# First batch of a packed-attention mixture-of-experts kernel: earlier splits, four hidden blocks as split products, and batch 1's key scores behind six items instead of two

## The chip, the cores and the metric

The kernel runs on one core of a Trainium2 chip. The metric is the device time of one execution in microseconds. Its engines are TensorE (PE, with its weight loads PEld), VectorE (DVE), ScalarE (ACT), GpSimd (POOL) and SyncE (SP, a queue of loads and stores).

## The reference

For each of 8 batches and 8 heads (576 tokens, head width 64) 32 packing queries `p` attend over keys `k` and values `v`; then the tokens' queries `q` attend over these 32 packed rows. The result (4608 x 512) goes through a layer of 8 experts, of which each token takes the best.

```python
p_packed = sm_attn(p, k, v)          # 32 rows for each head
out = sm_attn(q, p_packed, p_packed)
x = out.transpose(0, 2, 1, 3).reshape(4608, 512)
logits = (x / norm(x)) @ en.T / tau  # 8 experts
e = argmax(logits); gate = softmax(logits)[e]
y = gate * (relu(x @ w1[e]) @ w2[e]) # 512 -> 1024 -> 512
```

## The kernel before, in words

The kernel guesses one expert for a whole batch, works with that expert's weights, and would do the tokens that chose another in a rest loop. It never forms `x`: with the probabilities AT (for each group of four heads 128 packed rows by 576 tokens) and G = packed rows times w1 (128 x 1024 for each group), the hidden layer is relu(G^T AT). A batch's feed-forward, `ffn`, is 16 items `hidden(hf, f)`: two halves of 288 tokens and eight blocks f of 128 hidden columns. Then come `h4`, the leftover rows' second layer (tokens beyond 512, L924), and four row blocks of the second layer (L940).

Products come in two forms. A split product takes each operand as a high part (a cast to fp32r) and a low part (the remainder) and sums three products, high x high, high x low, low x high: an item has two groups, so six products (L893). A plain fp32 product takes one instruction for each group and no splits (`first_half`, L872), which needs only `g32` (G before its split) and `ats` (AT before its split).

`split` makes such a pair: a cast on ACT (L274), and a subtraction on POOL or DVE (L275). `split_g` does one of four blocks of G (column half fc, group g), `split_w2` one of eight blocks of w2 (L785, L786), `high` and `low` the two parts of AT for a half (L619, L623).

The attention of batch b + 1 runs in between: key tiles are transposed on DVE (`flip`, L285 to L287), key scores on PE (L260), maximum and exponential (L350, L355), p1 turned (L370) and copied (L381, L384), values (L390), query tiles transposed (L290, L294). `route` computes for each of five token blocks the squares and logits (L680, L689, L696) from AT and `ppx`, packed rows with 16 logits columns behind them, split too (`rows_split`, `logits_split`).

In the first batch all of this is started from a cold state, and a table sets the order. `PLAN[n + 1]` is what is emitted behind step n of `ffn`: s is a step of the first batch's softmax (its order in `ORDS`), G a `split_g`, a a step of batch 1's attention, w a `split_w2`, q and r steps of the first batch's logits and route. `ENG` says which of the subtractions go to POOL (p) and which to DVE (v): places 0 to 5 are S0, S1, N0, N1, L0, L1, places 6 to 9 the four `split_g`. All engines execute in the order emitted.

Banks set further waits: four PSUM banks of tag `pf` hold items until the second copy on DVE (L898, and L903 in the second half) has read them, two double banks of tag `pb` serve scores, turns and route. Six buffers `nat` hold loaded tiles until they are transposed.

Of the kernel before, what the change touches and what calls it, by code (L numbers as in the profile page):

```python
# [18 lines left out]
HB = 4  # L19
# [4 lines left out]
def kernel(  # L24
# [16 lines left out]
    NG = H // HB  # L41
# [230 lines left out]
    def split(dst, src, eng=nc.gpsimd):  # L272

        nc.scalar.copy(dst[0], src)  # L274
        eng.tensor_tensor(out=dst[1], in0=src, in1=dst[0].bitcast(F32), op=ALU.subtract)  # L275
# [278 lines left out]
    def att2(x, after=None, first=False, early=False):  # L554

        def eng(name, hf):
            i = ("S0", "S1", "N0", "N1", "L0", "L1").index(name + str(hf))
            return nc.gpsimd if first and ENG[i] == "p" else nc.vector

# [72 lines left out]
        def softmax():  # L632
# [4 lines left out]
            if first:  # L637
# [3 lines left out]
                groups = {"": both, "a": slice(0, 1), "b": slice(1, 2)}  # L641
                order = [(names[t[0]], int(t[1]), groups[t[2:]]) for t in ORDS.split()]
            for step, hf, *gs in order:
# [135 lines left out]
    def split_w2(x):  # L779
        f = len(x.w2s)  # L780
        if f == NF:
            return
        t = sb.tile([P, 2, DM], F32R, name="w2s", tag="w2s", bufs=NF)
        raw = x.w2r[f // 2][:, f % 2, :]
        nc.scalar.copy(t[:, 0], raw)  # L785
        nc.gpsimd.tensor_tensor(out=t[:, 1], in0=raw, in1=t[:, 0].bitcast(F32), op=ALU.subtract)  # L786
        x.w2s.append(t)

    PASSES = ((0, 0), (0, 1), (1, 0))

    def split_g(x):
        fc, g = x.gs // NG, x.gs % NG
        x.gs += 1
        split(
            [x.G[:, a, g, fc * 512 : fc * 512 + 512] for a in range(2)],
            x.g32[fc][:, g],
            nc.gpsimd if ENG[5 + x.gs] == "p" else nc.vector,
        )
# [32 lines left out]
    def ffn(x, store, late=False, after=None, end=False):  # L831
# [34 lines left out]
        opened = {}  # L866

        def first_half(f, g):

            if g == 0:  # L870
                opened[f] = ps.tile([P, 512], F32, name="pf", tag="pf")
            nc.tensor.matmul(  # L872
                opened[f][:, :HS], x.g32[f // 4][:, g, f % 4 * P : f % 4 * P + P],
                x.ats[0][:, g], start=(g == 0), stop=(g == NG - 1),
            )

        def hidden(hf, f):
            cs = slice(hf * HS, (hf + 1) * HS)

            assert not late or hf == 0 or x.soft and x.gs >= NG * (f // 4 + 1)  # L880
            if late and hf == 0:
                for g in range(f in opened, NG):
                    first_half(f, g)
                pf = opened[f]
            else:
                pf = ps.tile([P, 512], F32, name="pf", tag="pf")
                ops = [
                    (x.G[:, a, g, f * P : (f + 1) * P], x.AT[:, m, g, cs])
                    for g in range(NG)
                    for a, m in PASSES  # L890
                ]
                for n, (w, r) in enumerate(ops):
                    nc.tensor.matmul(pf[:, :HS], w, r, start=(n == 0), stop=(n == len(ops) - 1))  # L893
            yield
            n = HS if hf == 0 else 512 - HS
            cs = slice(hf * HS, hf * HS + n)
            nc.scalar.activation(hT[:, 0, f, cs], pf[:, :n], AF.Relu)  # L897
            nc.vector.scalar_tensor_tensor(  # L898
                out=hT[:, 1, f, cs], in0=pf[:, :n], scalar=0.0,
                in1=hT[:, 0, f, cs].bitcast(F32), op0=ALU.max, op1=ALU.subtract,  # L900
            )
            if hf:
                nc.vector.tensor_scalar(  # L903
                    out=h4[:, f], in0=pf[:, n:HS], scalar1=0.0, scalar2=None, op0=ALU.max
                )
            if f % 2 and not late:
                split_w2(x)
# [9 lines left out]
        for hf in range(2):  # L917
            for f in range(NF):
                yield from hidden(hf, f)
# [13 lines left out]
        for c in range(4):  # L933

            w = 256 if end and c == 3 else 512
            for at in range(0, 512, w):
                pf = ps.tile([P, 512], F32, name="pf", tag="pf")
                for f in range(NF):
                    for i, (a, m) in enumerate(PASSES):
                        nc.tensor.matmul(  # L940
# [254 lines left out]
    def store_main(b):  # L1195
# [24 lines left out]
    GATE = 18  # L1220


    ORDS = "U0a B0a S0a X0a U0b B0b T0a S0b X0b T0b N0a N0b R0a U1 B1 S1 X1 R0b T1 N1 R1 H1 L1 H0 L0"
    ENG = "pvpppppppp"

    PLAN = (
        "qssq", "sssssssss", "sss", "ss", "ss", "ssG", "", "sG", "ssa", "ssa",
# [82 lines left out]
    with tc.If(n_rest > 0):  # L1312
        with tc.For_i(0, B, 1) as b:
            nb = nc.values_load(rest_i[0:1, ds(b, 1)], min_val=0, max_val=S)
            with tc.If(nb > 0):
                x = Batch()
# [43 lines left out]
                for c in range(NC5):  # L1360
                    for hf in range(2):
                        a = acc[hf][:, c] if c < 4 else acc[0][64 * hf : 64 * hf + 64, 4]
# [38 lines left out]
```

## Time and profile before

| | |
|---|---|
| median of 3 runs | 445.36 us (444.05 to 445.59) |
| profiled execution | 444.3 us, span from first to last instruction 442.6 us |
| PE busy | 430.8 us, 97% of the span |
| DVE, ACT, POOL busy | 303.3, 203.6, 150.2 us |
| mean granted clock of TensorE | 0.996 of full speed |
| HBM traffic | 78.00 MB read, 9.44 MB written |

PE is the engine that is nearly always busy. Its records overlap (a product starts while the one before it still drains), so distances between starts, not busy times, tell how fast it works. The chain that ended last is 89% PE and 6% DMA; the DMA part lies in the first 23 us, before the first G.

### The profile page before, as it was taken

How to read it: one execution, taken by the hardware profiler on the slowest of the kernel's cores; microseconds unless marked ns; L12 is line 12 of the kernel's file. 1: busy time of each engine (PE TensorE's matmuls, PEld its weight loads, DVE VectorE, ACT ScalarE, POOL GpSimd, SP SyncE). 2: the span in 40 equal slices, each digit the busy share in tenths (PEclk: the TensorE clock that was granted, in tenths of full speed). 3: DMA queues.
4: the chain of work that ended last, by engine and by line, in shares of the span. 5: the costliest groups of instructions: out<-in, count | busy, mean ns of one | idle time of the engine just before them, and what ended most of it. 6: DMA issues, size and time to landing. Idle time of an engine off the chain costs nothing.

```text
span 442.6 us, 10441 instructions
## 1 busy us (share of the span) xinstructions
PE 430.8 (97%) x3762; PEld 339.4 (77%) x3763; DVE 303.3 (69%) x1006; ACT 203.6 (46%) x477; POOL 150.2 (34%) x201
## 2 busy tenths in 40 slices
PE   8799999999999999999999999999999999999994
PEld 6537768798787978879687977879687886879784
DVE  5568759669965899469883799558994698535400
ACT  2457632773237723465127723366235751466110
POOL 2538645342404441152504523044501534035000
PEclk9999999999999999999999999999999999999998
DMA  7999988877985479944995389843998206500011
GB/s 208 290 282 286 232 213 325 246 180 204 321 301 141 110 216 360 275 113 138 298 364 143 88 231 353 268 128 102 241 386 243 79 1 220 221 26 24 15 48 54
DMA packets 40267, 88.22 MB, mean 199 GB/s; under 512 B 10312, under 2 KB 19848, under 8 KB 40208
## 3 DMA queue, kind: packets, MB, share of 16 engines
q1 hardware_dynamic: 31920, 57.96, 46.2%
q0 software_dynamic: 8000, 29.43, 18.3%
q8 instruction: 32, 0.52, 0.5%
q14 instruction: 27, 0.22, 0.2%
q10 hardware_dynamic: 288, 0.08, 0.1%
HBM read 78.00 MB, written 9.44 MB: 198 GB/s over the span
## 4 chain that ended last, share of the span: by engine, by line
PE 89%; DMA 6%; DVE 2%; ACT 1%; SPq 1%; issue 0%; DVEq 0%; ACTq 0%
PE pf L940 41%; PE pf L893 21%; PE pf L924 6%; PE pt L680 6%; PE pt L260 4%; PE pt L810 3%; PE pt L390 3%; DMA nat<-in_v 2%; DMA nat<-in_q 2%; PE pt L370 1%; DMA w1t<-in_moe_w 1%; PE pf L853 1%; DVE hT L898 1%; PE pt L853 1%; PE pf L872 0%; SPq L201 0%
## 5 line engine op out<-in xcount | busy, mean ns | idle before, releaser
L940 PE MATMUL pf<-w2s,hT 128*128 128x512 f32 (+1 forms) x792 | 189.1, 390 | 0.0
L940 PEld LDWEIGHTS pf<-w2s,hT 128*128 128x128 f32 x792 | 142.1, 188 | 37.4 <-issue 6.7
L786 POOL TENSOR_TENSOR w2s<-w2r,w2s 128x512 fp32r<-128x512 f32 x64 | 82.6, 1292 | 178.3 <-ACT w2s L785 176.6
L893 PE MATMUL pf<-AT,G 128*128 128x288 f32 x720 | 105.0, 299 | 0.1
L893 PEld LDWEIGHTS pf<-AT,G 128*128 128x128 f32 x720 | 97.5, 188 | 5.1 <-issue 2.3
L897 ACT ACTIVATE hT<-pf 128x224 fp32r<-128x224 f32 (+1 forms) x128 | 48.1, 388 | 43.7 <-PE pf L893 42.4
L898 DVE SCALAR_TENSOR_TENSOR hT<-pf,hT 128x224 fp32r<-128x224 f32 (+1 forms) x128 | 52.4, 414 | 16.3 <-ACT hT L897 16.3
L696 ACT ACTIVATE at<-pt 128x512 f32<-128x512 f32 (+1 forms) x40 | 23.9, 598 | 40.9 <-DVE lg L689 40.2
L785 ACT CAST w2s<-w2r 128x512 fp32r<-128x512 f32 x64 | 39.8, 623 | 1.2 <-issue 1.2
L1200 ACT ACTIVATE o<-pf,gate 128x512 f32<-128x512 f32 (+1 forms) x41 | 26.0, 634 | 29.2 <-PE pf L940 18.6
L680 PEld LDWEIGHTS pt<-ppx,AT 128*128 128x128 f32 (+1 forms) x240 | 33.2, 177 | 6.0 <-ACT at L696 1.4
L680 PE MATMUL pt<-ppx,AT 128*128 128x264 f32 (+1 forms) x240 | 36.4, 287 | 0.5
L924 PE MATMUL pf<-w2r,h 128*64 128x256 f32 x256 | 34.1, 390 | 0.0
L689 DVE TENSOR_REDUCE lg<-pt 128x8 f32<-128x16 f32 (+1 forms) x40 | 6.9, 171 | 36.4 <-PE pt L680 36.4
L290 DVE STREAM_TRANSPOSE kt<-nat 128x512 f32<-128x512 f32 x28 | 31.2, 1120 | 0.0
L824 DVE TENSOR_TENSOR G<-pt,G 128x512 fp32r<-128x512 f32 x28 | 18.8, 688 | 14.4 <-ACT G L823 14.4
L592 ACT ACTIVATE st<-st 128x576 f32<-128x576 f32 (+1 forms) x17 | 11.2, 658 | 30.1 <-DVE st L589 29.4
L275 POOL TENSOR_TENSOR ppx<-pp,ppx 128x256 fp32r<-128x256 f32 x16 | 11.5, 739 | 38.7 <-ACT ppx L274 38.7
L924 PEld LDWEIGHTS pf<-w2r,h 128*64 128x64 f32 x256 | 15.7, 136 | 9.8 <-issue 4.3
L619 ACT CAST AT<-at 128x576 fp32r<-128x576 f32 x16 | 10.8, 673 | 20.3 <-DVE at L613 20.3
L775 POOL DMA_DIRECT2D w2r<-in_moe_w x28 | 19.7, 712 | 0.0
L823 ACT CAST G<-pt 128x512 fp32r<-128x512 f32 x28 | 15.8, 588 | 7.1 <-DVE G L824 4.5
(181 smaller groups left out, 479.9 us busy)
## 6 DMA issues: line engine op xcount, KB each, us to landing
nat<-in_k SPq DMA_DIRECT2D x112, 140.0 KB, 3.4
nat<-in_q SPq DMA_DIRECT2D x112, 140.0 KB, 4.0
w1t<-in_moe_w POOLq DMA_DIRECT2D x14, 1024.0 KB, 8.3
w2r<-in_moe_w POOLq DMA_DIRECT2D x28, 512.0 KB, 11.1
out<-o SPq DMA_DIRECT2D x27, 256.0 KB, 3.3
nat<-in_v SPq DMA_DIRECT2D x32, 160.0 KB, 4.1
nat<-in_v SPq DMA_DIRECT2D x32, 128.0 KB, 4.1
w1t<-in_moe_w SPq DMA_DIRECT2D x4, 512.0 KB, 6.1
```

Source lines behind the costliest of these rows:

```text
L290: nc.vector.transpose(kt[:, :512].rearrange("p (c i a) -> p c a i", a=4, i=32), t[:, :16].rearrange("p (c a) d -> p c a d", a=4),)
L680: nc.tensor.matmul(pt[:r, 512 * g : 512 * g + XW], AT[:, a, g, c * P : c * P + r], x.ppx[:, m, g], start=(i == 0), stop=(i == 2),)
L696: nc.scalar.activation(scr[:r, :, : HB * D], ptv[:r, :, 0 : HB * D], AF.Square, accum_out=ss[:r, c : c + 1])
L775: queue.dma_start(t, w2e[:, 2 * i : 2 * i + 2, :])
L785: nc.scalar.copy(t[:, 0], raw)
L786: nc.gpsimd.tensor_tensor(out=t[:, 1], in0=raw, in1=t[:, 0].bitcast(F32), op=ALU.subtract)
L893: nc.tensor.matmul(pf[:, :HS], w, r, start=(n == 0), stop=(n == len(ops) - 1))
L897: nc.scalar.activation(hT[:, 0, f, cs], pf[:, :n], AF.Relu)
L898: nc.vector.scalar_tensor_tensor(out=hT[:, 1, f, cs], in0=pf[:, :n], scalar=0.0, in1=hT[:, 0, f, cs].bitcast(F32), op0=ALU.max, op1=ALU.su ...
L924: nc.tensor.matmul(pf[64 * hf : 64 * hf + 64, :256], h4[:, f], x.w2r[f // 2][:, f % 2, hf * 256 : hf * 256 + 256], start=(f == 0), stop=(f ...
L940: nc.tensor.matmul(pf[:, :w], hT[:, a, f, c * P : (c + 1) * P], x.w2s[f][:, m, at : at + w], start=(f == 0 and i == 0), stop=(f == NF - 1 ...
L1200: nc.scalar.activation(o[:, :w], pf[:, :w], AF.Copy, scale=x.gate[:, c : c + 1])
```

## The change

The four blocks of G are split in the order (1, 0), (0, 0), (1, 1), (0, 1) of (fc, g) instead of (0, 0), (0, 1), (1, 0), (1, 1), and earlier. AT's first half is split (H0, L0) before the second (H1, L1), earlier too, with both low parts on DVE instead of POOL. Items f4 to f7 of the first half become split products. The rest of the table moves with that: batch 1's steps later, w2's splits elsewhere.

```diff
+    GORD = ((1, 0), (0, 0), (1, 1), (0, 1))
     def split_g(x):
-        fc, g = x.gs // NG, x.gs % NG
+        fc, g = GORD[x.gs]
...
-            assert not late or hf == 0 or x.soft and x.gs >= NG * (f // 4 + 1)
-            if late and hf == 0:
-                for g in range(f in opened, NG):
-                    first_half(f, g)
+            assert not late or hf == 0 and (f < HB or x.gs > 2) or x.soft and x.gs == 4
+            if f in opened and hf == 0:
+                first_half(f, 1)
                 pf = opened[f]
...
-    ORDS = "U0a B0a S0a X0a U0b B0b T0a S0b X0b T0b N0a N0b R0a U1 B1 S1 X1 R0b T1 N1 R1 H1 L1 H0 L0"
-    ENG = "pvpppppppp"
+    ORDS = "U0a B0a S0a X0a U0b B0b T0a S0b X0b T0b N0a N0b R0a U1 B1 S1 X1 R0b H0 T1 L0 N1 R1 H1 L1"
+    ENG = "pvppvvpppp"
...
-        "qssq", "sssssssss", "sss", "ss", "ss", "ssG", "", "sG", "ssa", "ssa",
+        "qssq", "sssssssss", "sss", "ssG", "ssGsss", "sG", "", "", "s", "G",
```

On PE the stretch behind the plain products of f3 reads, before the change, as follows. The items' banks are `pf`, f4 to f7 of the first half the first four rows, then f0 and f1 of the second half; L260 is the start of batch 1's key scores.

```order
L872 MATMUL pf_576<-at_501,g32_473 128x288 x2
L872 MATMUL pf_590<-at_501,g32_473 128x288 x2
L872 MATMUL pf_604<-at_501,g32_473 128x288 x2
L872 MATMUL pf_618<-at_501,g32_473 128x288 x2
L893 MATMUL pf_627<-AT_452,G_469 128x288 x6
L893 MATMUL pf_640<-AT_452,G_469 128x288 x6
L260 MATMUL pt_647<-kt_570,pw_562 32x288 x2
```

And with the change, from f4 on:

```order
L893 MATMUL pf_560<-AT_452,G_469 128x288 x6
L893 MATMUL pf_571<-AT_452,G_469 128x288 x6
L893 MATMUL pf_594<-AT_452,G_469 128x288 x6
L893 MATMUL pf_607<-AT_452,G_469 128x288 x6
L893 MATMUL pf_625<-AT_452,G_469 128x288 x6
L893 MATMUL pf_647<-AT_452,G_469 128x288 x6
L893 MATMUL pf_666<-AT_452,G_469 128x288 x6
L893 MATMUL pf_679<-AT_452,G_469 128x288 x6
L893 MATMUL pf_689<-AT_452,G_469 128x288 x6
L893 MATMUL pf_702<-AT_452,G_469 128x288 x6
L260 MATMUL pt_709<-kt_601,pw_589 32x288 x2
```

f4 to f7 have six products each, and the key scores stand behind six items of the second half, not two.

On ACT, ahead of the first square of the route (L696), before: the last w2 cast ahead of the last item's copy, the two copies of p1T, m1 (the packed rows' logits) and its cast into ppx.

```order
L785 CAST w2s_762<-w2r_465 128x512
L897 ACTIVATE hT_470<-pf_747 128x224
L381 COPY p1T_777<-pt_756 128x512
L381 COPY p1T_780<-pt_771 128x512
L443 COPY m1_788<-pu_783 128x16
L274 CAST ppx_291<-m1_788 128x2x8
L785 CAST w2s_817<-w2r_465 128x512
L696 ACTIVATE at_821,ss_807<-pt_810 128x2x256
```

After:

```order
L897 ACTIVATE hT_470<-pf_747 128x224
L355 ACTIVATE p1_771,sums_772<-pt_710,mx_760 128x576
L274 CAST ppx_291<-pp4_401 128x256
L443 COPY m1_794<-pu_789 128x16
L785 CAST w2s_796<-w2r_465 128x512
L381 COPY p1T_807<-pt_783 128x512
L381 COPY p1T_810<-pt_801 128x512
L785 CAST w2s_813<-w2r_467 128x512
L274 CAST ppx_291<-m1_794 128x2x8
L785 CAST w2s_820<-w2r_467 128x512
L696 ACTIVATE at_847,ss_826<-pt_829 128x2x256
```

m1's cast stands behind the second exponential, the second half of ppx, both copies of p1T and two w2 casts; all w2 casts stand ahead of the squares.

On POOL the difference between the two (- before, + after), from the normalization of the second half (L604) on:

```order
-L604 TENSOR_TENSOR st<-st,s_531 128x576
-L275 TENSOR_TENSOR G<-g_472,G 128x512 x2
-L623 TENSOR_TENSOR AT<-at_542,AT 128x2x288
-L623 TENSOR_TENSOR AT<-at,AT 128x2x288
-L275 TENSOR_TENSOR G<-g_473,G 128x512 x2
-L786 TENSOR_TENSOR w2s<-w2r,w2s 128x512
+L275 TENSOR_TENSOR G<-g_473,G 128x512
+L275 TENSOR_TENSOR G<-g_472,G 128x512
+L604 TENSOR_TENSOR st<-st,s_534 128x576
+L275 TENSOR_TENSOR G<-g_473,G 128x512
+L275 TENSOR_TENSOR G<-g_472,G 128x512
+L786 TENSOR_TENSOR w2s<-w2r,w2s 128x512 x3
```

Two blocks of G go ahead of the normalization, and AT's low parts (L623) are gone from POOL; further on seven of the eight w2 splits stand ahead of m1's remainder, five before.

## Rows read from the trace of the kernel before

**Rows 1.** Windows of busy time of the whole kernel: the stretch in us and its length, then for PE, PEld, DVE, ACT and POOL the busy us and, in brackets, the instructions, then the granted clock of TensorE (1.00 is 2.4 GHz, 0.50 is 1.2 GHz), the busy share of the DMA engines and GB/s.

```profile
20.00:23.10 3.10, 1.63 (x23) 0.69 (x21) 1.87 (x4) 1.45 (x4) 0.67 (x1) 1.00 0.97 324
59.00:439.00 380.00, 377.54 (x3206) 304.20 (x3204) 264.71 (x846) 172.19 (x400) 119.38 (x149) 1.00 0.62 192
439.00:442.60 3.60, 0.00 (x0) 0.00 (x0) 0.00 (x0) 0.00 (x0) 0.00 (x0) 0.50 0.03 7
```

**Rows 2.** Order of time, merged, of PE from 21 to 72 us (the row at 50.30 from a window that begins there): start in us, length from the first start to the last end, engine, line, operation, tiles, shape, the number of records, and in brackets idle time before it with what ended it. A plain fp32 product has two records.

```profile
23.13 3.07 PE L853 MATMUL pf<-w1t,tw 64*32 64x512 f32 x16 [0.77 <-DMA w1t<-in_moe_w]
...
30.95 4.34 PE L872 MATMUL pf<-at,g 128*128 128x288 f32 x16
...
37.87 2.20 PE L893 MATMUL pf<-AT,G 128*128 128x288 f32 x12
40.00 1.20 PE L260 MATMUL pt<-kt,pw 64*32 64x288 f32 x32
41.13 5.07 PE L893 MATMUL pf<-AT,G 128*128 128x288 f32 x36
46.03 0.71 PE L370 MATMUL pt<-ident,p 128*128 128x128 f32 x5
...
50.30 0.88 PE L680 MATMUL pt<-ppx,AT 128*128 128x264 f32 x5
...
52.85 1.00 PE L680 MATMUL pt<-ppx,AT 128*128 128x264 f32 x6
53.78 0.65 PE L924 MATMUL pf<-w2r,h 128*64 128x256 f32 x4
...
56.52 0.65 PE L924 MATMUL pf<-w2r,h 128*64 128x256 f32 x4
57.10 1.73 PE L390 MATMUL pt<-nat,p1T 128*32 128x64 f32 x80
...
59.03 1.66 PE L940 MATMUL pf<-w2s,hT 128*128 128x512 f32 x6
```

**Rows 3.** Order of time, merged, of DVE, same columns, 32 to 42 us.

```profile
32.51 0.46 DVE L898 SCALAR_TENSOR_TENSOR hT<-pf,hT 128x288 fp32r<-128x288 f32 x1 [2.62 <-ACT hT L897]
...
36.25 0.42 DVE L898 SCALAR_TENSOR_TENSOR hT<-pf,hT 128x288 fp32r<-128x288 f32 x1
...
37.39 0.42 DVE L898 SCALAR_TENSOR_TENSOR hT<-pf,hT 128x288 fp32r<-128x288 f32 x1
...
40.68 0.21 DVE L903 TENSOR_SCALAR h<-pf 128x64 f32<-128x64 f32 x1
...
41.11 0.21 DVE L903 TENSOR_SCALAR h<-pf 128x64 f32<-128x64 f32 x1
```

**Rows 4.** Order of time, merged, of ACT, same columns, 27 to 32 us.

```profile
27.91 0.68 ACT L592 ACTIVATE st<-st 128x576 f32<-128x576 f32 x1 [1.08 <-DVE st L589]
30.20 0.59 ACT L863 COPY g<-pt 128x512 f32<-128x512 f32 x1 [1.61 <-PE pt L853]
...
31.55 0.62 ACT L274 CAST G<-g 128x512 fp32r<-128x512 f32 x1
```

**Rows 5.** Instructions of DVE and POOL that split, shift or scale: first by line over the whole kernel (count, durations in ns as least/median/most, first and last start in us, shape), then rows of the order of time, one of DVE and two of POOL.

```profile
L623 DVE TENSOR_TENSOR AT<-at,AT x14: 694/726/761, 75.2 to 381.4; 128x576 fp32r<-128x576 f32 x14
L301 DVE TENSOR_SCALAR pbd<-pn x7: 217/221/918, 33.9 to 330.9; 128x128 f32<-128x128 f32 x7
L275 POOL TENSOR_TENSOR ppx<-m,ppx x8: 232/236/748, 50.0 to 365.4; 128x16 fp32r<-128x16 f32 x8
L275 POOL TENSOR_TENSOR G<-g,G x4: 1275/1286/1300, 32.2 to 39.1; 128x512 fp32r<-128x512 f32 x4
L589 DVE TENSOR_TENSOR st<-st,mx x15: 694/758/1057, 27.1 to 375.3; 128x576 f32<-128x576 f32 x15
...
71.57 1.06 DVE L589 TENSOR_TENSOR st<-st,mx 128x576 f32<-128x576 f32 x1
...
70.56 1.45 POOL L275 TENSOR_TENSOR ppx<-pp,ppx 128x256 fp32r<-128x256 f32 x2
71.95 0.75 POOL L275 TENSOR_TENSOR ppx<-m,ppx 128x16 fp32r<-128x16 f32 x1
```

**Rows 6.** Order of time of the queue of loads (SP), two single issues: the first of the third q tile, and the first of the second v tile of batch 1.

```profile
40.90 0.35 SPq L175 DMA_DIRECT2D nat<-in_q  x1
...
48.05 0.38 SPq L201 DMA_DIRECT2D nat<-in_v  x1
```

**Rows 7.** Order of time, merged, of DVE and of ACT from 41 to 49 us: steps between batch 1's key scores and the route.

```profile
41.24 0.75 DVE L350 TENSOR_REDUCE mx<-pt 128x1 f32<-128x576 f32 x1
...
44.15 0.15 DVE L362 TENSOR_SCALAR ri<-sums 128x1 f32<-128x1 f32 x1 [0.20 <-ACT p L355]
...
43.29 0.74 ACT L355 ACTIVATE p<-pt,mx 128x576 f32<-128x576 f32 x1
43.91 0.20 ACT L355 ACTIVATION_READ_ACCUMULATOR p<-pt,mx 128x1 f32 x1
...
48.38 1.08 ACT L381 COPY p1T<-pt 128x512 f32<-128x512 f32 x2
```

**Rows 8.** List of waits from 46.0 to 59.1 us: who waited for whom, us in total, times, longest.

```profile
PEld pt L680 <- ACT ppx L274: 0.6, 1, 0.6
...
PEld pt L680 <- POOL ppx L275: 0.3, 1, 0.3
```

More of the change, by code (lines that the diff above doesn't have):

```diff
@@ L1220 @@
     GATE = 18
-    ORDS = "U0a B0a S0a X0a U0b B0b T0a S0b X0b T0b N0a N0b R0a U1 B1 S1 X1 R0b T1 N1 R1 H1 L1 H0 L0"
-    ENG = "pvpppppppp"
+    ORDS = "U0a B0a S0a X0a U0b B0b T0a S0b X0b T0b N0a N0b R0a U1 B1 S1 X1 R0b H0 T1 L0 N1 R1 H1 L1"
+    ENG = "pvppvvpppp"
     PLAN = (
-        "qssq", "sssssssss", "sss", "ss", "ss", "ssG", "", "sG", "ssa", "ssa",
[2 rows of a table removed]
+        "qssq", "sssssssss", "sss", "ssG", "ssGsss", "sG", "", "", "s", "G",
+        "ss", "a", "sa", "a", "aw", "a", "w", "", "w", "aa",
+        "aqw", "aaw", "aq", "aqw", "aw", "qw", "rk", "rkrk", "rkrr", "arrrr",
         "g", "ag", "g", "ag", "gaaa", "aa", "ga", "ga", "ga", "a",
```

2 rows, old and new, of the table PLAN are left out of this document.

## Prediction, made before the changed kernel ran

> **What bounds the kernel now.** The windows of busy time [rows 1] come first. From 59 us to 439 TensorE (PE) is busy 377.5 of 380 us at a granted clock of 1.00, and its list of waits is empty there: whatever moves PE's entry into that stretch moves the end by as much. That entry is the first second-layer product (L940) at 59.03 us [rows 2]. The change touches nothing after it but buffer numbers, and nothing before 25 us. So the question is when L940 starts, and what counts is PE's order of work from 33 to 59 us.
>
> The merged order of PE [rows 2] cuts that stretch. The four items f4 to f7 of the first half run from 33.0 to 37.87, the eight items of the second half and batch 1's key scores (L260) to 46.03, then transposes, leftover rows (L924), route products (L680) and values (L390). The work itself is less than the time. A plain fp32 item is four records; 16 records take 4.34 us, less 0.41 for the last one's end, so 0.26 a record and 1.05 an item. A split item is six records; 36 take 5.07, less 0.29, so 0.137 a record and 0.82 an item. f4 to f7 should take 4.2 us and take 4.8; the eight second-half items 6.6, with L260 7.7, and take 8.16.
>
> VectorE's (DVE) order says why [rows 3]. An item's bank is free only after its second copy (L898), and between two of these stands one transposition of a key tile: 36.25 to 37.39 is 1.14 us. PE waits for that cadence, not for itself. In the second half a copy goes with one for the leftover rows (L903), 0.43 for both, 40.68 to 41.11, where the copy alone is 0.34; with a key tile that makes 1.23.
>
> **The change, part by part.**
>
> *f4 to f7 as split products.* Four times 1.05 less 0.82: at most 0.92 us of PE. An item that starts after a pause takes 0.91.
>
> *Casts and low parts before them.* The first split item now needs, ahead of its products, AT's high and low part of the first half and both G blocks of its column half. ScalarE (ACT) waited 1.08 us before 27.91 and 1.61 before 30.20 [rows 4]: the cast of G (1,0) fits at 26.9, of (0,0) at 28.5, of AT at 29.0 to 29.7 (0.62 each as the G cast at 31.55, the last a little longer); the copies of g32 at 30.2 and 31.06 stay. The cover is ACT's waiting, for DVE and for PE. DVE's low part of AT takes 0.73 [rows 5] and lies in the 2.62 us in which DVE idled before 32.51 [rows 3]. GpSimd (POOL) does G (1,0) from 27.6, (0,0) to 30.5, the normalization to at most 32.3, G (1,1) 32.4 to 33.7 and (0,1) 33.8 to 35.1, 1.29 each [rows 5]; its own two low parts of AT are gone. One cast stays in front of the first copies on ACT: f0's copy ends on DVE at 33.09, where it ended 32.97. f4 starts at 33.14 (was 33.02), its last product, which needs G (1,1), just finds it ready; f7 ends at 36.45 (was 37.8).
>
> *The second low part on DVE.* It stands behind f3's copy, at 34.84, and ahead of f4's, whose bank the second half's first item waits for. Its price alone is 0.73 [rows 5]. But POOL then splits G (0,1) until 35.08, and three rows show these two engines not running such work side by side [rows 5]: L589 took 1.06 at 71.57 where its median is 0.76, beside a POOL subtraction that lasted to 72.01; the small POOL subtraction after it took 0.75 where its median is 0.24; and L301 once took 0.92 where 0.22 is usual, its only run of seven in the stretch where POOL splits G. I take the same here: done at 35.73, 0.65 after POOL's end as L589 was, against 35.57 unhindered. The bounds are 0 and 0.45 of delay (L589 at its 1.06 plus what is queued); the price is 0.16.
> The Trainium skill, page "SBUF — State Buffer", section "SBUF: two separate sides", says that a DVE instruction with two SBUF inputs and a GpSimd one that reads SBUF exclude each other for the whole instruction. By that rule the delay is also the rest of POOL's instruction, about 0.24, and without it the sum would be 0.16 smaller; the L589 row sides with the rule.
>
> *What DVE's order makes of it.* f4's copy ends at 36.07, then L301 (0.22 now, POOL waits for ACT) and L302, f5's at 36.89; at 1.14 each f6 38.03 and f7 39.17; at 1.23 the second half's first two 40.39 and 41.62. PE takes the second half's items at 36.45, 37.25, 38.08, and then on DVE's releases of f7 and of the first two: 39.22, 40.44, 41.67, to 42.6. So most of the 0.92 goes back into that wait. Key tiles are done 1.2 us later; they free buffers for loads of q and v. The load queue gets to these only later [rows 6]: the first tile is free at 37.7, in time for the third q tile's issue at 40.90, the last at 41.2, in time for v's second at 48.05. Hidden.
>
> *Key scores later.* L260 takes 1.13 [rows 2], now at 42.67 instead of 40.00. Two items follow, to 45.5: 0.55 us earlier than the 46.03 of before. But the second batch's softmax hangs on these scores and starts 2.7 us later, and it is a chain in which each step waits for the other engine [rows 7]: maximum on DVE 0.75 (to 44.63), exponential and its sum on ACT 0.82, behind the copy of item f6 (to 46.0), 1/sum on DVE in two steps of 0.15 (46.39), the second maximum 0.75 (47.08), the second exponential 0.82 (47.94), PE's transposes (done 48.75). PE fills this with leftover rows f0 to f2, the first transposes and the logits rows; it stands still from 47.9 only until 48.0, then does f3 and f4 to 49.55.
>
> *What stands ahead of the route.* The route's first products need the 16 logits columns of ppx split: high part by ACT, low part by POOL. Before, PE waited 0.6 for that cast and 0.3 for the remainder [rows 8]. Now ACT has, in order: m1's copy, a w2 cast, both p1T copies, a w2 cast, then this one. Both p1T copies hang on the late chain: 48.77 to 49.85; the w2 cast ends at 50.34, m1's at 50.43. POOL takes w2's low part first, 50.42 to 51.7 (1.29 for this size [rows 5]), then the remainder, to 51.89. PE's second route product, which reads it, goes at 51.95 instead of 50.30 [rows 2]: PE waits about 0.8 and then 1.2 us. What is queued behind on PE is all else; POOL's last w2 split and memset have time.
>
> *From there to L940.* Before: 50.30 to 59.03, 8.73. After: the rest of the first route tile 0.81 (six products at 0.12, and a changeover), then twice a leftover item and two tiles, a last item, values and counts. An item alone takes 0.58 (56.52 to 57.10), a tile after a changeover 0.83 (52.85 to 53.78 less the changeover at its end), the next one 0.82 with it, values and counts 1.93 (57.10 to 59.03) [rows 2]: 0.81 + 3 x 0.58 + 2 x 1.65 + 1.93 = 7.78. A query transposition still stands between two logit sums on DVE, as before, but no w2 cast among the squares that free the banks; by the steps' prices one wait of 0.07 is left. L940 at 59.8.
>
> **Sum.** 45.5 for 46.03 is -0.55; the route's late start makes it +1.65; the shorter rest (7.85 for 8.73: one item and the waits) takes back 0.88: +0.8. The profiled execution took 444.3 us (span 442.6), so 445.1. The median of the runs shown, 445.36, lies 1.06 above the profiled one, so I forecast 446.2 for the median. Half a per cent, 2.2 us, is about what a measurement of this kernel can tell from no change: this is no change.
>
> **Rivals.**
>
> *The route is not late.* If the chain of softmax steps runs shorter than I put it, or POOL comes to the logits columns before w2's split, PE goes on from the leftover rows at 49.55 after no more than the 0.6 that it once waited for ACT, and with 7.85 behind that L940 starts at 58.1. That is -0.9, 444.4. For it: PE waited for these columns only 0.9 in all before [rows 8], so a shorter chain would hide them. Against: the order on ACT and POOL is fixed, and each step's price is a row.
>
> *The split items gain nothing.* If DVE's cadence holds already from f4 on (the low part held up by both POOL splits, 0.45 and more), the second half ends at 46.0 to 46.3 and all behind it with it: L940 at 60.3 to 60.6, 446.8.
>
> *Gain throughout.* Route not late, and half a microsecond of DVE's waits gone too: -1.5, 443.9. The change would then do what moving work into gaps can at best.
>
> *Slower: the clock falls.* PE does one product between 49.55 and 51.95. Should the granted clock go to 1.2 GHz after that, the 7.8 us of products up to L940 would take twice as long while it lasts: half of them are +3.9, all +7.8 on top of the forecast, so 450.1 to 454.0. It decides only if the pause is long enough to drop the clock. Against it: before 23.13 PE waited 0.77 for a load [rows 2], it worked 1.63 of 3.10 us from 20.0 on, and the granted clock stayed 1.00; the one fall is at the end, with PE idle [rows 1].
> The Trainium skill's "TensorE: Matmul & The Clock Gate", Part 1, has the clock halved when the engine has been idle. No run here shows it inside a kernel; the trace agrees only in that the fall at 439 comes after PE's last product.
>
> **Numbers.** The forecast's case 0.56 (its own range 445.4 to 447.0); route not late 0.20; no gain from the items 0.14; gain throughout 0.04; clock 0.04; 0.02 for what I don't see. The runs shown spread by 1.5 us, so a part of the outer cases falls beyond a bound. Faster by over 0.5% (below 443.1): 0.05. Slower (above 447.6): 0.08. Between: 0.87. The range reaches from the case without a late route to beyond the one without a gain, 444.1 to 447.8.
>
> **What would show it.** Right: f4's first split product at 33.1 and f7's end near 36.5; PE waiting for DVE's copies at 39.2, 40.4 and 41.7; the second low part on DVE longer than 0.73; L260 at 42.7; the first two route products more than a microsecond apart, with POOL's ppx split as releaser at 51.9; L940 at 59.8, and after it the same distances as before. Wrong: L940 at 58.6 or earlier, or later than 60.8; a granted clock under 1.00 between 50 and 60; f4 waiting for a G split; a change of more than 0.5 us after L940.

## The result: 0.57% slower, inside the range and three times the forecast loss

The changed kernel takes 446.98 us (median of 7 runs, 446.36 to 448.28), the kernel before in the same comparison 444.32 (443.91 to 445.59): ratio 1.0057, 95% interval 1.0042 to 1.0071. That is 2.7 us, where +0.8 was forecast; the forecast of 446.2 lies nearer only because it was added to the 445.36 of the three runs then known, and that part is luck. The profiled execution took 447.5 us with a span of 445.8, 3.2 more than before. L940 starts 3.08 us later, and the distances behind it are as before (445.8 - 62.11 = 383.7; before 442.6 - 59.03 = 383.6). So all of the loss lies before 62 us. Not all of it need be the change: L1146, the scores from which the first batch's softmax hangs, starts at 21.92 here and at 21.28 before; it differs from execution to execution (21.0 to 22.6 in the ten traces of this case). Here the granted clock is one reason, in work that the change leaves as it was: it is 0.59 from 16 to 20 us, and 13 transposing products (L1136) ahead of these scores take 2.91 us, where they take 1.58 at a clock of 1.00 in the run m1_first below. Little of it reaches the later steps: m1_first and filled, whose work up to 46 us is that of the changed kernel, have L1146 at 21.06 and 22.23, and the key scores (L260) at 43.36 and 43.60.

### The profile page after: what moved, and what is told of

The parts are those of the page before. It is cut to its first block, busy times and chain, and to the rows that moved or that the text cites. A ratio compares the mean times of both kernels' runs of the same rounds, so it can differ in the third digit from the quotient of the medians.

```text
span 445.8 us, 10459 instructions
## 1 busy us (share of the span) xinstructions
PE 432.1 (97%) x3770; PEld 342.7 (77%) x3771; DVE 306.4 (69%) x1008; ACT 204.2 (46%) x477; POOL 147.8 (33%) x199
## 4 chain that ended last, share of the span: by engine, by line
PE 92%; DVE 2%; ACT 2%; DMA 2%; issue 1%; POOL 0%; SPq 0%; ACTq 0%
PE pf L940 41%; PE pf L893 21%; PE pt L680 7%; PE pf L924 7%; PE pt L260 4%; PE pt L811 3%; PE pt L390 3%; PE pt L370 2%; DMA nat<-in_q 2%; PE pf L1049 1%; PE pt L238 1%; PE pf L1136 1%; ACT p L355 1%; PE pu L433 0%; PE pu L419 0%
## 5 line engine op out<-in xcount | busy, mean ns | idle before, releaser
L940 PE MATMUL pf<-w2s,hT 128*128 128x512 f32 (+1 forms) x792 | 189.2, 390 | 0.0
L940 PEld LDWEIGHTS pf<-w2s,hT 128*128 128x128 f32 x792 | 142.2, 188 | 37.4 <-issue 6.7
L893 PE MATMUL pf<-AT,G 128*128 128x288 f32 x744 | 108.9, 299 | 1.1 <-POOL G L275 0.6
L893 PEld LDWEIGHTS pf<-AT,G 128*128 128x128 f32 x744 | 100.8, 188 | 6.7 <-issue 2.8
L898 DVE SCALAR_TENSOR_TENSOR hT<-pf,hT 128x224 fp32r<-128x224 f32 (+1 forms) x128 | 52.2, 413 | 12.8 <-ACT hT L897 12.8
L696 ACT ACTIVATE at<-pt 128x512 f32<-128x512 f32 (+1 forms) x40 | 23.9, 597 | 43.1 <-DVE lg L689 42.4
L680 PEld LDWEIGHTS pt<-ppx,AT 128*128 128x128 f32 (+1 forms) x240 | 34.3, 184 | 7.0 <-POOL ppx L275 1.2
L680 PE MATMUL pt<-ppx,AT 128*128 128x264 f32 (+1 forms) x240 | 37.4, 294 | 1.6 <-POOL ppx L275 1.0
```

What stands on the lines that cost most here:

```text
L680: nc.tensor.matmul(pt[:r, 512 * g : 512 * g + XW], AT[:, a, g, c * P : c * P + r], x.ppx[:, m, g], start=(i == 0), stop=(i == 2),)
L696: nc.scalar.activation(scr[:r, :, : HB * D], ptv[:r, :, 0 : HB * D], AF.Square, accum_out=ss[:r, c : c + 1])
L898: nc.vector.scalar_tensor_tensor(out=hT[:, 1, f, cs], in0=pf[:, :n], scalar=0.0, in1=hT[:, 0, f, cs].bitcast(F32), op0=ALU.max, op1=ALU.su ...
L940: nc.tensor.matmul(pf[:, :w], hT[:, a, f, c * P : (c + 1) * P], x.w2s[f][:, m, at : at + w], start=(f == 0 and i == 0), stop=(f == NF - 1 ...
```

## The profile after, from 21 us to L940

PE's merged order of time answers to [rows 2]; columns as there. All line numbers from L853 on are one higher, or the same from L893.

```profile
21.92 0.72 PE L1146 MATMUL pt<-spare,tw 64*32 64x288 f32 x16 [0.73 <-ACT spare L1139]
...
33.28 0.92 PE L893 MATMUL pf<-AT,G 128*128 128x288 f32 x5
34.83 6.41 PE L893 MATMUL pf<-AT,G 128*128 128x288 f32 x43 [0.63 <-POOL G L275]
...
43.64 1.20 PE L260 MATMUL pt<-kt,pw 64*32 64x288 f32 x32
...
46.56 1.08 PE L924 MATMUL pf<-w2r,h 128*64 128x256 f32 x8
...
51.39 0.39 PE L680 MATMUL pt<-ppx,AT 128*128 128x264 f32 x1 [0.52 <-ACT ppx L274]
52.81 0.87 PE L680 MATMUL pt<-ppx,AT 128*128 128x264 f32 x5 [1.04 <-POOL ppx L275]
...
54.20 2.97 PE L680 MATMUL pt<-ppx,AT 128*128 128x264 f32 x12
...
62.11 1.66 PE L940 MATMUL pf<-w2s,hT 128*128 128x512 f32 x6
```

f4 starts about where it was forecast (33.28, forecast 33.14), does five of its six products and then waits for G (1,1). The key scores (L260) start at 43.64, forecast 42.67; the second half is done at 46.56, later than the 46.03 of before. PE then waits twice ahead of the route's second product, at 52.81 instead of 50.30. Twelve products take 2.97 us at 54.20, where 1.7 to 2.0 is usual. The windows of busy time, columns as in [rows 1], say why these take so long:

```profile
50.00:52.00 2.00, 1.25 (x9) 0.47 (x5) 1.54 (x4) 1.85 (x5) 1.88 (x2) 1.00 0.83 165
52.00:54.00 2.00, 1.19 (x9) 0.86 (x9) 0.37 (x4) 0.07 (x1) 2.00 (x3) 1.00 0.34 91
54.00:56.00 2.00, 2.00 (x12) 1.80 (x9) 1.19 (x3) 0.62 (x2) 0.14 (x3) 0.57 0.79 223
56.00:58.00 2.00, 2.00 (x11) 1.20 (x9) 1.99 (x5) 1.22 (x4) 0.00 (x0) 0.58 0.23 46
58.00:60.00 2.00, 2.00 (x18) 1.59 (x16) 0.91 (x5) 0.88 (x5) 0.00 (x0) 1.00 0.86 260
```

From 54 to 58 us, behind the pause that ended at 52.81, the granted clock is 0.57 and 0.58, so for most of that time at the lower level, 1.2 GHz. DVE's order of time answers to [rows 3] and to the L589 and L623 of [rows 5]:

```profile
27.76 1.24 DVE L589 TENSOR_TENSOR st<-st,mx 128x576 f32<-128x576 f32 x1
...
30.54 1.06 DVE L599 TENSOR_SCALAR s<-s 128x18 f32<-128x18 f32 x1
...
35.07 1.56 DVE L623 TENSOR_TENSOR AT<-at,AT 128x576 fp32r<-128x576 f32 x1
36.55 0.45 DVE L898 SCALAR_TENSOR_TENSOR hT<-pf,hT 128x288 fp32r<-128x288 f32 x1
```

And POOL's:

```profile
27.12 1.27 POOL L275 TENSOR_TENSOR G<-g,G 128x512 fp32r<-128x512 f32 x1 [0.43 <-ACT G L274]
30.31 1.26 POOL L275 TENSOR_TENSOR G<-g,G 128x512 fp32r<-128x512 f32 x1 [1.92 <-ACT G L274]
32.05 1.48 POOL L604 TENSOR_TENSOR st<-st,s 128x576 f32<-128x576 f32 x1 [0.48 <-DVE s L600]
33.49 2.53 POOL L275 TENSOR_TENSOR G<-g,G 128x512 fp32r<-128x512 f32 x2
...
49.91 2.67 POOL L786 TENSOR_TENSOR w2s<-w2r,w2s 128x512 fp32r<-128x512 f32 x2
52.54 0.22 POOL L275 TENSOR_TENSOR ppx<-m,ppx 128x16 fp32r<-128x16 f32 x1
```

Three DVE instructions lie across a POOL split and are long: L589 1.24 us (its median over the kernel is 0.76), L599 1.06 (median 0.18), L623 1.56 (median 0.73). L589 ends at 29.00 and L623 at 36.63, each 0.61 after POOL's split (28.39 and 36.02). In the kernel before the scaling on DVE and the normalization on POOL stood free:

```profile
29.42 0.18 DVE L599 TENSOR_SCALAR s<-s 128x18 f32<-128x18 f32 x1
30.07 1.16 POOL L604 TENSOR_TENSOR st<-st,s 128x576 f32<-128x576 f32 x1 [4.01 <-DVE s L600]
```

The holds delay the normalization (L604, start 32.05), G (1,1) behind it, and f4. The normalization itself takes 1.48 us, 0.32 more than before; DVE's first low part (L623, 31.82 to 32.51) now lies beside it. The remainder of the logits columns, 0.22 us of work at 52.54, stands behind two w2 splits.

## Experiments

The theory after this reading has three parts: POOL's splits hold DVE's softmax steps (L589, L599) and the second low part; the late split of the logits columns makes PE wait; and the granted clock falls behind that wait. Starts in us from each profiled execution, names as in the headings below ("done" is the start of the first row behind the second half's items; the route's second product stands one step of 0.13 behind the start where all six are one row). Ratios are against the runs of before in the same comparison (its medians there are 444.32, 444.57 and 444.36):

| kernel | L1146 | L260 | 2nd half done | route's 2nd product | L940 | median, us | ratio to before (95%) |
|---|---|---|---|---|---|---|---|
| before | 21.28 | 40.00 | 46.03 | 50.30 | 59.03 | 444.36 (31 runs) | |
| changed | 21.92 | 43.64 | 46.56 | 52.81 | 62.11 | 446.98 | 1.0057 (1.0042 to 1.0071) |
| m1_first | 21.06 | 43.36 | 46.28 | 50.65 | 58.68 | 444.34 | 0.9991 (0.9980 to 1.0002) |
| late_m1_alone | 21.26 | 40.00 | 46.04 | 52.86 | 63.86 | 448.03 | 1.0074 (1.0060 to 1.0089) |
| filled | 22.23 | 43.60 | 46.52 | 52.79 | 60.82 | 446.17 | 1.0038 (1.0021 to 1.0055) |
| low1_pool | 22.55 | 44.24 | 47.16 | 53.41 | 61.44 | 446.65 | 1.0046 (1.0031 to 1.0061) |
| g_behind_n1 | 22.00 | 44.33 | 47.25 | 53.51 | 61.54 | 448.52 | 1.0089 (1.0076 to 1.0102) |
| g_held | 22.02 | 43.25 | 46.18 | 50.54 | 58.58 | 444.11 | 0.9991 (0.9978 to 1.0004) |
| order_a | 21.00 | 42.54 | 45.46 | 49.83 | 57.86 | 443.43 | 0.9978 (0.9965 to 0.9991) |
| order_b | 21.50 | 42.49 | 45.41 | 49.77 | 57.82 | 443.37 | 0.9979 (0.9966 to 0.9992) |

In filled, g_held and the two orders the line numbers are up to five higher (L590, L600, L605, L624, L903 are L589, L599, L604, L623, L898).

**m1_first: the late split of the logits columns taken out.** Entries 20 to 29 of the table:

```diff
-        "aqw", "aaw", "aq", "aqw", "aw", "qw", "rk", "rkrk", "rkrr", "arrrr",
+        "aqw", "aaw", "aq", "aq", "qa", "", "rwk", "rkwrk", "rkrr", "arrrrw",
```

> The changed kernel, with one thing moved: the 16 logits columns of ppx are split right behind m1's copy, ahead of both copies of p1T, and the last three w2 splits follow later, among the route's steps. Theory (the late split of these columns makes PE stand, and the stand makes the granted clock fall): the second route product starts at 50.9 us or earlier instead of 52.81, PE stands less than 1 us ahead of it, the granted clock stays 1.00 from 50 to 60 us, L940 starts 1.5 us earlier where only the wait goes and up to 3 us earlier where the clock's fall goes too: 443.7 to 445.4 us where the changed kernel takes 447. Rival (the second batch's softmax chain holds the route, whoever splits the columns): the products still wait, now for the copies of p1T or for the squares behind them, and L940 moves by less than 0.5 us. Second rival (the three w2 splits now stand in the way among the squares): the wait at 52 goes, but at least 1 us of it comes back between the route's products.

PE's order of time around the route:

```profile
50.52 1.00 PE L680 MATMUL pt<-ppx,AT 128*128 128x264 f32 x6
...
58.68 1.66 PE L940 MATMUL pf<-w2s,hT 128*128 128x512 f32 x6
```

No wait is left, and the time is that of before: 2.6 us (446.98 - 444.34) come from this one move. The three w2 splits among the squares cost nothing. All that the changed kernel does before 46 us, the split items and the early splits, gains nothing: the second half is done at 46.28, before at 46.03, though L1146 is 0.22 earlier here.

**late_m1_alone: the late split by itself, in the kernel before.**

```diff
-        "aw", "aw", "aq", "k", "q", "rwrkw", "k", "rk", "rrr", "arrrrw",
+        "aw", "aw", "aq", "k", "wwq", "rrk", "k", "rk", "rrr", "arrrrw",
```

> The kernel before, with one part of the change alone: the split of the 16 logits columns stands behind two more w2 splits; items, G, low parts and key scores stay as before. Theory (this part costs by itself): the second route product starts 1.5 to 2.5 us later than the 50.30 of before, L940 1 to 2 us later, 445.3 to 446.3 us where before takes 444.3, and about 1.4 us more if the granted clock falls after the wait. Rival (it is the late key scores that make the route late, and with early key scores the split is hidden): second route product within 0.5 us of 50.30, the same time as before.

PE's order of time, and windows:

```profile
50.74 0.39 PE L680 MATMUL pt<-ppx,AT 128*128 128x264 f32 x1 [1.03 <-ACT ppx L274]
52.86 2.79 PE L680 MATMUL pt<-ppx,AT 128*128 128x264 f32 x11 [1.74 <-POOL ppx L275]
...
63.86 1.43 PE L940 MATMUL pf<-w2s,hT 128*128 128x512 f32 x5
```

```profile
52.00:54.00 2.00, 1.14 (x5) 1.14 (x6) 0.00 (x0) 0.00 (x0) 0.94 (x4) 0.58 0.80 229
54.00:56.00 2.00, 2.00 (x10) 1.64 (x11) 1.63 (x4) 0.69 (x2) 0.00 (x0) 0.50 0.31 71
56.00:58.00 2.00, 2.00 (x10) 0.99 (x7) 1.83 (x5) 0.69 (x2) 0.00 (x0) 0.50 0.58 168
58.00:60.00 2.00, 2.00 (x12) 1.38 (x11) 0.18 (x1) 0.52 (x2) 0.00 (x0) 0.71 0.88 239
```

The route is 2.56 us late with early key scores too, so the place in ACT's and POOL's order makes it late, not the key scores. PE waits 2.77 us in all, the granted clock is 0.50 from 54 to 58 us and 0.58 and 0.71 in the stretches around, and from the second product to L940 it takes 11.00 us: 8.73 in the kernel before. The loss, 3.5 us by the medians, is larger than I had put it. In the profiled execution, the longest of the six (449.31; the others 446.94 to 448.62), L940 is 4.83 us late, 2.56 by the route's start and 2.27 behind it, where the clock is low. With m1_first and the changed kernel this makes a square: the late split costs 2.6 us in the one kernel and 3.5 in the other, everything else about nothing.

**filled: PE kept at work in the wait.** In the route's first product of batch 0:

```diff
+                    again = 10 if x is bat[0] and c == g == i == 0 else 0
+                    for _ in range(again):
+                        nc.tensor.matmul(
+                            pt[:r, :XW], AT[:, a, g, :r], x.ppx[:, m, g], start=True, stop=True
+                        )
```

> The changed kernel with nothing moved: only the first route product, which PE does before it waits for the logits columns' low part, is repeated ten times more (about 1.2 us of the same product), so that PE works in most of the wait. Theory (the granted clock falls because PE stands there, and a part of the changed kernel's loss is that fall): the second route product starts within 0.2 us of 52.81, the granted clock is 1.00 from 52 to 60 us, the way from there to L940 is 8.0 us, where it was 9.30 in the profiled execution of the changed kernel; no execution above 447.2 us, median 446.2 to 446.9. Rival (the clock falls by another cause, or the pause ahead of the first route product is enough): stretches at 0.5 to 0.6 remain in some executions, and times of 447.5 to 448.5 beside 446.4.

```profile
52.00:54.00 2.00, 2.00 (x17) 1.59 (x16) 0.37 (x4) 0.08 (x1) 1.98 (x3) 1.00 1.07 231
54.00:56.00 2.00, 2.00 (x18) 1.68 (x16) 1.83 (x4) 1.11 (x4) 0.14 (x2) 1.00 1.12 258
56.00:58.00 2.00, 1.99 (x15) 1.39 (x14) 1.71 (x6) 1.07 (x5) 0.00 (x0) 1.00 0.72 191
```

The wait is the same (second product near 52.8; the row of repeats and the next hide its own start), the clock is 1.00 throughout, and the way to L940 is 8.03 us, as in m1_first. The median falls by 0.8 us, to 446.17; the longest of 8 runs is 447.30, and three of the changed kernel's 7 are above that. That fits a fall that hangs on PE standing still, but only the times speak for it: one trace at 1.00 does not show it, since the fall does not come in each execution. low1_pool and g_behind_n1 have the same pause, and their profiled executions keep 1.00 and need 8.03 us. Where it comes it costs 9.30 - 8.03 = 1.27 us. What decides between the two is open, and a pause of this length isn't needed for a fall: before the one at 16 to 20 us (0.59 in the changed kernel's trace, 0.64 in filled's) no wait of PE from 8 us on is longer than 0.60 us.

**low1_pool: the second low part back on POOL.**

```diff
-    ENG = "pvppvvpppp"
+    ENG = "pvppvppppp"
```

> The changed kernel, with AT's second low part given back to GpSimd, behind both G splits. Theory (VectorE's low part is held up by GpSimd's G splits, 1.56 us where 0.73 is its own): f4's copy starts 1.4 us or more earlier than 36.55, the key scores start 0.9 to 1.6 us earlier than 43.64, and L940 moves by 0.9 us or by what the late split of the logits columns leaves of it. Rival one (the low part costs its own 0.73 only, the rest is f4's wait for G): key scores 0.3 to 0.7 us earlier. Rival two (the split of the logits columns sets the route's start in any case): key scores earlier, but the second route product still within 0.4 us of 52.81 and the time the same.

DVE's order of time, and a row of POOL's:

```profile
35.95 0.46 DVE L898 SCALAR_TENSOR_TENSOR hT<-pf,hT 128x288 fp32r<-128x288 f32 x1 [0.65 <-ACT hT L897]
36.32 1.42 DVE L301 TENSOR_SCALAR pbd<-pn 128x128 f32<-128x128 f32 x1
38.01 0.42 DVE L898 SCALAR_TENSOR_TENSOR hT<-pf,hT 128x288 fp32r<-128x288 f32 x1
```

```profile
36.23 1.42 POOL L623 TENSOR_TENSOR AT<-at,AT 128x576 fp32r<-128x576 f32 x1
```

f4's copy does come 1.2 us earlier after L1146 (35.95 - 22.55 = 13.40; 36.55 - 21.92 = 14.63). But now L301 meets the low part on POOL: 1.42 us instead of 0.21, and it ends with it. f5's copy, 38.01 - 22.55 = 15.46, is where it was (37.40 - 21.92 = 15.48), and so is L260. L1146 is a loose reference, as said above, but by the clock of the trace nothing comes earlier either: L260 starts at 44.24, where it was 43.64. My theory's gain failed; its mechanism moved on to the next instruction, which I had not priced. The time is within its uncertainty that of the changed kernel.

**g_behind_n1: all G splits behind the normalization.**

```diff
-    GORD = ((1, 0), (0, 0), (1, 1), (0, 1))
+    GORD = ((1, 0), (1, 1), (0, 0), (0, 1))
...
-        "qssq", "sssssssss", "sss", "ssG", "ssGsss", "sG", "", "", "s", "G",
+        "qssq", "sssssssss", "sss", "ss", "sssss", "sGG", "", "", "sG", "G",
```

> The changed kernel, with all four splits of G behind the normalization of the second half, in the order (1,0), (1,1), (0,0), (0,1), so that no GpSimd split lies beside VectorE's softmax steps. Theory (a VectorE instruction that reads two SBUF tensors or runs in its fast form does not run beside a GpSimd split): the subtraction L589 that took 1.24 us at 27.76 takes 0.76 again, the scaling L599 that took 1.06 at 30.54 takes 0.18 to 0.3, the normalization L604 starts at 30.9 or earlier instead of 32.05; f4's sixth product, which now needs the second split behind it, starts between 34.0 and 34.8 as in the changed kernel, and the time moves by less than 1 us. Rival (these two were long for another reason, the load of keys or their own queue): 1.2 and 1.0 us as before, and L604 not earlier than 31.8.

```profile
27.85 0.76 DVE L589 TENSOR_TENSOR st<-st,mx 128x576 f32<-128x576 f32 x1
...
30.15 0.18 DVE L599 TENSOR_SCALAR s<-s 128x18 f32<-128x18 f32 x1
...
35.02 1.58 DVE L623 TENSOR_TENSOR AT<-at,AT 128x576 fp32r<-128x576 f32 x1
...
36.88 0.95 DVE L301 TENSOR_SCALAR pbd<-pn 128x128 f32<-128x128 f32 x1
```

```profile
30.79 1.45 POOL L604 TENSOR_TENSOR st<-st,s 128x576 f32<-128x576 f32 x1 [4.01 <-DVE s L600]
32.21 5.54 POOL L275 TENSOR_TENSOR G<-g,G 128x512 fp32r<-128x512 f32 x4
```

Without a POOL split beside them L589 takes 0.76 and L599 0.18, and the normalization starts 1.26 us earlier. But four splits then run until 37.75, across L623 (1.58) and L301 (0.95). The four take 5.54 us where four alone take 4 x 1.27 = 5.08: DVE's instruction slips in between two of them and POOL waits too. The time is 1.5 us worse than the changed kernel's, more than I expected; L260 is 0.7 later, and the profiled execution, at 447.0, is the shortest of five: the other four (448.2 to 448.7) have a mean granted clock of 0.988 to 0.992, this one 0.999, so a fall of the clock is likely in them, but no trace of theirs shows it or where it lies.

**g_held: one split held back by a token on POOL.** m1_first and, ahead of the first split:

```diff
+        if x.gs == 0:
+            held = sm.tile([P, 1], F32, name="held", tag="held", bufs=1)
+            mx = x.mxs[1][:, 0, :1]
+            nc.gpsimd.tensor_tensor(out=held, in0=mx, in1=mx, op=ALU.subtract)
```

> The kernel with the logits columns split first, plus one thing: GpSimd does a tiny subtraction on VectorE's maxima before its first G split, so that the split can't start before VectorE's subtraction L589 does. Nothing else moves. Theory (whichever of the two engines starts first holds the other): L589 takes 0.76 to 0.85 us instead of 1.80, the G split is stretched or starts late, VectorE's scaling L599 then comes ahead of the second G split and takes 0.2 instead of 1.07, the normalization starts 0.3 to 0.6 us earlier after the query scores (L1146) than 10.7 us, f4's sixth product and L940 move by the same 0.3 to 0.6: 443.8 us where the kernel without it takes 444.3. Rival (L589's length has nothing to do with GpSimd): 1.2 to 1.8 us again, and no gain.

```profile
27.86 0.76 DVE L590 TENSOR_TENSOR st<-st,mx 128x576 f32<-128x576 f32 x1
...
30.16 1.07 DVE L600 TENSOR_SCALAR s<-s 128x18 f32<-128x18 f32 x1
```

```profile
27.91 0.76 POOL L798 TENSOR_TENSOR held<-mx 128x1 f32<-128x1 f32 x1 [1.11 <-DVE mx L584]
28.63 2.57 POOL L275 TENSOR_TENSOR G<-g,G 128x512 fp32r<-128x512 f32 x2
```

L589 starts first and takes 0.76; now POOL is the one that stands, 0.76 us for one number in each partition. So the exclusion works both ways, and who starts first wins. But the second split follows at once and lies across L599, which takes 1.07 as before. No gain that can be measured: half of the theory's step was missed, since the second split was free to start early.

**order_a and order_b: the splits in another order.** order_a is m1_first with the token, G in the order (1,0) | normalization | (1,1), (0,0), the second low part on POOL, (0,1), and L301 moved from behind f4's copy to the start of the softmax, some 15 us earlier. order_b has G (0,0) in the first place and subtracts (1,0) on DVE. The core of order_b's edit to m1_first, beside the token:

```diff
-    GORD = ((1, 0), (0, 0), (1, 1), (0, 1))
+    GORD = ((0, 0), (1, 0), (1, 1), (0, 1))
-    ENG = "pvppvvpppp"
+    ENG = "pvppvppvpp"
-        "qssq", "sssssssss", "sss", "ssG", "ssGsss", "sG", "", "", "s", "G",
-        "ss", "a", "sa", "a", "aw", "a", "w", "", "w", "aa",
+        "qssq", "asssssssss", "sss", "ssG", "sssssG", "sG", "", "", "sG", "ss",
+        "", "a", "sa", "a", "aw", "", "w", "", "w", "aa",
```

> The kernel with the logits columns split first, and the first 14 us of the splits in an order that keeps GpSimd's work away from VectorE's: G (1,0) held as in the experiment before, the other three G blocks behind the normalization in the order (1,1), (0,0), (0,1), AT's second low part on GpSimd between the last two, and batch 1's scaling of the packing queries (L301) long before, at 21 us. Theory (the items f4 to f7 gain nothing because VectorE's copies are held up by GpSimd's splits and f4 by G (1,1)): no wait for G at f4's sixth product, no VectorE instruction over 0.9 us between 27 and 40 us, L260 by 0.7 to 1.5 us earlier than 43.36 and L940 as much earlier than 58.68: 442.9 to 443.7 us. Rival (VectorE's own cadence of copy and key tile bounds the stretch whatever GpSimd does): L260 within 0.4 us of 43.36 and no gain over 444.3.

> As the run before, but G (0,0) is the block that GpSimd does ahead of the normalization, and G (1,0) is subtracted on VectorE in its idle time behind the first low part; GpSimd then has two G blocks and the second low part behind the normalization, all done by 36.5 us. Theory (what is late for the second half's items is GpSimd's last block): second half starts at 36.5 to 37 us, L260 1 to 1.8 us earlier than 43.36, L940 as much earlier than 58.68: 442.5 to 443.3 us. Rival (VectorE's G block is held by the normalization on GpSimd and pushes the first copies back): f0's copy later than 33.0 us and f4 with it, no better than the run before.

order_b's DVE, then its PE:

```profile
29.64 0.18 DVE L600 TENSOR_SCALAR s<-s 128x18 f32<-128x18 f32 x1
...
30.65 1.64 DVE L275 TENSOR_TENSOR G<-g,G 128x512 fp32r<-128x512 f32 x1
32.56 0.82 DVE L903 SCALAR_TENSOR_TENSOR hT<-pf,hT 128x288 fp32r<-128x288 f32 x2 [0.27 <-ACT hT L902]
```

```profile
33.07 7.42 PE L898 MATMUL pf<-AT,G 128*128 128x288 f32 x48
...
42.49 1.20 PE L260 MATMUL pt<-kt,pw 64*32 64x288 f32 x32
...
57.82 1.66 PE L945 MATMUL pf<-w2s,hT 128*128 128x512 f32 x6
```

Both are the fastest here, 0.22% under the kernel before, about 1 us; order_a lies in its expectation, order_b just above its own (its L260 is 0.87 us earlier than m1_first's, forecast 1 to 1.8) and no better than order_a. f4 to f7 and four items of the second half run as one row of 48 products. The second half is done at 45.41, 0.62 earlier than before: a gain ahead of the route now reaches the end. How much of it the split items bring and how much the moves do isn't separated: L301 and L302, which took 0.48 us between the copies of f4 and f5 in the changed kernel (36.92 to 37.40), and the second low part no longer lie between DVE's copies in either run. DVE's G split was held by the normalization (1.64 us, where L623, an eighth larger, takes 0.73), but in DVE's idle time, so that the first copy starts at 32.56, as in the kernel before (32.51, [rows 3]). Not free is L301's new place: in order_a it waited 1.73 us there for its load.

## Why the prediction's range held, and which of its steps did not

The median lies in the range, but three of the four signs of being wrong that I had named came: L940 later than 60.8, a granted clock under 1.00 between 50 and 60 us, and f4 waiting for a G split. The forecast's "this is no change" fell as well: the interval of the ratio, 1.0042 to 1.0071, lies clear of 1. That the range holds the median is owed to its width and to the high median that it was worked out from.

*The last step of the sum* was right: whatever moves L940 moves the end.

*f4 to f7 as split products, and "most of the 0.92 goes back".* The cadence was right: f5 to f7's copies start at 37.40, 38.55 and 39.69, 1.15 and 1.14 apart, and the first two of the second half, at 40.83 and 42.04, stand 1.21 apart. But the second half was forecast to be done at 45.5, 0.55 us earlier than before, and was at 46.56, in m1_first at 46.28. The rival in which the items gain nothing (46.0 to 46.3) was nearest here, with 46.56 beyond it; I gave it 0.14.

*The step that failed there* is "casts and low parts before them", which I costed at nothing with ACT's waiting as the cover, "for DVE and for PE". I named POOL's splits at 27.6 and to 30.5, and did not ask which DVE instruction lies beside them: L589 and L599, with 0.5 and 0.9 us of hold, on the chain to the normalization. Nor did I price that the first low part beside the normalization makes that longer, 1.48 us for 1.16. It was to end at 32.3 and ended at 33.53, 1.23 late. So "just finds it ready" became a wait of 0.63 for G (1,1). The same exclusion was priced for the second low part alone, and there POOL's end was taken at 35.08; it came at 36.02, and the hold was 0.83 instead of 0.16, beyond my bound of 0.45. (The 0.65 that I took from the L589 row for the end behind POOL's is 0.62 by that row, 71.57 + 1.06 - 72.01; here it was 0.61.) f4's copy gives way to L301 at 36.92, forecast 36.07, and L260 starts 0.97 late. L1146 is not the cause: in m1_first it is 0.22 earlier than before, the same holds are there (L589 took 1.80 us, L599 1.07), and L260 starts at 43.36 all the same. g_behind_n1 shows what L589 and L599 cost the normalization, 1.26 us. That the holds alone make the whole 0.97 isn't shown. order_b, with L1146 0.22 later than before and none of these holds, has L260 at 42.49 and the second half done at 45.41, near the forecast's 42.67 and 45.5, but it also has L301, L302 and the second low part out of the way. And filled reaches L260 at 43.60 with a second low part of only 0.83 us and no wait for G, because its first copies of f0 to f3 come some 0.7 us later (f0's at 33.52, in the changed kernel 32.76).
The Trainium skill, page "SBUF — State Buffer", section "Who interferes with whom", says that a DVE instruction with two SBUF inputs contends with a GpSimd one that reads SBUF, and so does one in a two-port mode, which `tensor_scalar` can enter, and that whoever issues first holds the shared ports for the whole instruction. The traces here agree for L589 and L623 (two inputs) and, by their lengths, for L301 and L599 (`tensor_scalar`; the mode itself no trace shows), and g_held shows the order of starting. I had used the rule for one instruction of the four.

*Behind the key scores* the steps were as priced. The chain from L260 to the second route product was forecast 42.67 to 51.95, 9.28 us, and took 43.64 to 52.81, 9.17. The split of m1 as the last of them, +1.65, was right in place and mechanism, if not in size: 2.51, of which L260's 0.97 is a part. It stood behind the copies of p1T and two w2 casts and splits, as told. The rival "the route is not late" fell.

*The rest to L940* was 7.85, and measured without a fall of the clock 8.03, with it 9.30. That it is shorter than the 8.73 of before fits the chain of before, which from 48.47 to 54.91 runs over a load of batch 1's values (3.91 us) and DVE's query transpositions; so the loads on that chain don't all lie in its first 23 us.

*The clock* was the rival that I gave 0.04, with a price of +3.9 to +7.8. The pause at 52 was in the forecast itself; what I held against the fall was a stretch with PE at work for 1.63 of 3.10 us [rows 1], which was no pause of this kind. The clock falls in some executions, and costs 1.3 us in the one profiled, less than the least that I had put: it was back by 58 us. The filled wait puts 0.8 us of the median on it; the two intervals overlap a little (1.0042 to 1.0071 and 1.0021 to 1.0055), so this is an estimate.
The Trainium skill's "TensorE: Matmul & The Clock Gate", section "HAM oscillation — how this bites in real kernels", tells of a kernel that waits for a load in each step and finds its clock halved after each wait. Halved clock behind a wait is what the traces of the changed kernel (0.57 behind 0.52 and 1.04 us) and of late_m1_alone show; those of low1_pool and g_behind_n1, with the same 0.52 and 1.04 us as the changed kernel, do not agree.

So of some 2.7 us, by the medians of three comparisons: 1.8 are the late route's wait (446.17 - 444.34), 0.8 the clock, and the rest of the change about nothing.

## What to carry to other kernels

A split put into GpSimd's idle time isn't free while VectorE subtracts or scales from SBUF: for each moved GpSimd instruction look up which VectorE instruction lies beside it at its new place, and which at the place to which it is pushed. A small step whose result stands at the head of TensorE's queue (here 16 columns, 0.2 us) goes ahead of all bulk work on both of its engines. A pause of TensorE is priced with a possible fall of the clock behind it.

## What I had not expected of the hardware

POOL and DVE exclude each other to the end, not in part: L589, 0.76 us long by itself, ended 0.61 us after POOL's split in the changed kernel, and a POOL subtraction of 128 x 1 took 0.76 us under L589. L599, a scaling of 128 x 18 numbers in place, went from 0.18 to 1.06 us. Transpositions on DVE weren't held: in the changed kernel L285 took 0.43 us at 37.74 with POOL idle and 0.42 at 38.89, beside a w2 split. And the same pause of PE, 0.52 and 1.04 us, was followed by a lower clock in the profiled execution of the changed kernel and by none in those of low1_pool and g_behind_n1; 1.03 and 1.74 us in late_m1_alone were followed by one. The changed kernel's trace has another fall, from 16 to 20 us, with no wait over 0.60 us in the 8 us ahead of it.
